# A conversion and two splits moved into a list scheduler's recurrence, two weight transposes moved to the host

## The chip, the core and the metric

One core of one Trainium2 chip runs the program. The metric is device time of one execution in microseconds (us). Engines are named as in the profile: PE is the matrix engine (TensorE), PEld its weight loads, DVE the vector engine, ACT the scalar engine, POOL the GpSimd engine, SP the engine that here only issues DMAs.

## The reference

Three layers follow one another, batch 4, 8 heads of 40 channels, 768 steps:

```python
# 1. recurrence, per batch and head, state 40 x 40
y[:, :, t] = einsum('bhd,bhde->bhe', r_t, state)
Sa = einsum('bhde,bhe->bhd', state, a_t)
state = state * w_t[:, :, None, :] - einsum('bhd,bhe->bhde', Sa, b_t) + einsum('bhd,bhe->bhde', v_t, k_t)
# x = y as [4, 768, 320]
# 2. four experts of causal attention (head dimension 64), the best two by x @ w_gate
out += mask_e * weight_e * (softmax(causal(q @ k.T / 8)) @ v @ wo[e])
# 3. gated MLP with a spatial product
h = maximum(x @ w_in, 0); u, v = h[..., :512], h[..., 512:]
vn = (v - mean(v)) / sqrt(var(v) + 1e-6)
return (u * (w_spatial @ vn + b_spatial)) @ w_out
```

w_in (320 x 1024) and w_out (512 x 320) arrive as float64; everything else is float32. The kernel receives the float64 arrays as 64-bit integers and makes float32 of them itself.

## The kernel before

**Recurrence.** `recurrence` works in 12 groups of 64 steps (group g, steps 2g and 2g+1 for the two halves of the batch). It describes each piece of work as an item: engine, assumed cost, due time, function, what it needs, the ring of buffers it takes from. `Plan.order` (line 53) is a list scheduler: it keeps a clock for each engine, looks at the items that could begin earliest, and of those takes the one with the smallest due time. What comes out is one order, in which all functions are called, so each engine's queue follows it. Items used below: `xo` (ACT issues the store of a solved block; the last one is ("xo", 11)), `gx` (SP loads G and R), `mb` (a product on PE), `mae`, `mbe`, `we`, `ue`, `ste`, `vte` (ACT's copies into G, xt, wsb, VU, s and vut), `u` (PE, line 324), `state` (DVE), `am` and `xs` (DVE; xs, line 418, makes the group's output), `out` (SP stores it to xd in DRAM, line 1072).

**Preparation in the tail.** Items of the plan know nothing of the attention weights. When ("xo", 11) has been issued, the early buffers are given back and a generator (`attn_prep`, line 600) is started: its first step issues all twelve loads of wq, wk, wv and w_gate on SP and a few small tiles; the rest, each a cast to a high part and a subtraction that leaves the low part, both on DVE (`split`, lines 586 to 593), is drawn eight steps at a time behind every `state`.

**Hand-over.** After the recurrence, `first_x` (line 727) loads the first batch's x as three tiles of 768 columns from xd (line 735) and splits them on DVE. Then attention and MLP of the four batches are written out in turns by `blend`, and the framework's scheduler sets the engines' order.

**First batch.** Beside attention(0) runs `rest`: `mlp_prep` and `wout_prep`. `mlp_prep` casts b_spatial (ACT) and takes its low part (POOL); loads wo and transposes it on PE into woT (line 680); for each of four column blocks of w_in loads three chunks (128, 128 and 64 rows of 256 columns), converts each with `load_f64`, multiplies by woT (line 691) and splits the result into wc_h and wc_l; for each of six row blocks of w_spatial transposes six 128 x 128 blocks on PE (line 703) and splits them from PSUM into ws_h and ws_l. All big inputs share one ring of four buffers, `big`. `wout_prep` converts four chunks of w_out (128 x 320) and splits them into wu_h and wu_l, the low part on POOL.

`load_f64` (line 557) is three words on ACT (scaled low word, sign, absolute value: lines 568, 569, 571), four integer or maximum forms on DVE (lines 572 to 575) and three products or sums on POOL (lines 576 to 578).

**Attention of a batch.** v for six row tiles (line 797, evicted into vv by ACT and DVE), then four heads e: projection (line 831), scores in blocks (first product line 859), maximum (DVE, 866), exponential (ACT, 871), scaling, transposes (901), product with vv (910, 912).

## Time and profile before

| what | us |
|---|---|
| median of three timed runs | 945.62 (943.25 to 946.6) |
| the profiled execution's own time | 940.45 |
| its span, first to last instruction | 938.7 |
| PE busy | 762.6 (81%) |
| DVE busy | 672.4 (72%) |
| ACT busy | 431.7 (46%) |
| POOL busy | 243.1 (26%) |
| first product of the first batch's attention | 404.44 |
| first product of the second batch's attention | 521.27 |
| mean granted clock of PE, share of full speed | 0.918 |

Times inside the execution count from the first instruction. A row's "idle before" names what ended the engine's idle time just before it. "issue" is time for which the profile shows no wait.

### The profile page before, as it was taken

How to read it: one execution, taken by the hardware profiler on the slowest of the kernel's cores; microseconds unless marked ns; L12 is line 12 of the kernel's file. 1: busy time of each engine (PE TensorE's matmuls, PEld its weight loads, DVE VectorE, ACT ScalarE, POOL GpSimd, SP SyncE). 2: the span in 40 equal slices, each digit the busy share in tenths (PEclk: the TensorE clock that was granted, in tenths of full speed). 3: DMA queues.
4: the chain of work that ended last, by engine and by line, in shares of the span. 5: the costliest groups of instructions: out<-in, count | busy, mean ns of one | idle time of the engine just before them, and what ended most of it. 6: DMA issues, size and time to landing. Idle time of an engine off the chain costs nothing.

```text
span 938.7 us, 29407 instructions
## 1 busy us (share of the span) xinstructions
PE 762.6 (81%) x12496; PEld 681.2 (73%) x12496; DVE 672.4 (72%) x1581; ACT 431.7 (46%) x1053; POOL 243.1 (26%) x425
## 2 busy tenths in 40 slices
PE   4615768968787878657887889998899988999898
PEld 4515667867676767645665779987799977999798
DVE  8999868889997943379988775576755767666730
ACT  2313433234343343136777554574655656555521
POOL 5652222232311010067810221111221113211041
PEclk9999898697989798868999989998899988999999
DMA  7956664677664352154101000010000100000001
GB/s 212 229 141 134 155 135 125 147 168 172 161 127 111 85 128 66 52 151 126 51 1 43 1 1 15 9 64 0 1 1 22 64 1 1 1 22 22 1 1 43
DMA packets 117669, 70.16 MB, mean 75 GB/s; under 512 B 100097, under 2 KB 103425, under 8 KB 117538
## 3 DMA queue, kind: packets, MB, share of 16 engines
q0 software_dynamic: 11520, 33.13, 12.5%
q1 hardware_dynamic: 54946, 25.71, 10.9%
q10 hardware_dynamic: 51072, 9.44, 5.5%
q8 instruction: 98, 1.61, 0.8%
q14 instruction: 33, 0.27, 0.1%
HBM read 50.95 MB, written 17.30 MB: 73 GB/s over the span
## 4 chain that ended last, share of the span: by engine, by line
PE 51%; DVE 27%; issue 7%; ACT 7%; DMA 4%; ACTq 1%; POOL 1%; SPq 1%; DVEq 0%; POOLq 0%
PE mm L942 6%; PE mm L943 6%; PE mm L944 5%; DVE sub L252 4%; PE mp L901 3%; DVE ls L254 3%; PE mp L831 3%; PE f L386 3%; PE pa L910 2%; PE f L411 2%; PE sc L859 2%; PE pa L912 2%; ACT f L871 2%; PE f L195 2%; DVE nm L866 2%
## 5 line engine op out<-in xcount | busy, mean ns | idle before, releaser
L871 ACT ACTIVATE f<-sc,nm 128x512 f32<-128x512 f32 (+3 forms) x128 | 68.9, 542 | 35.3 <-DVE nm L866 19.8
L195 PE MATMUL f<-at,kb 40*64 40x64 f32 x1536 | 41.4, 279 | 53.4 <-DVE kb L186 44.4
L592 DVE TENSOR_TENSOR ptl<-mp,pth 128x256 fp32r<-128x256 f32 (+2 forms) x144 | 65.3, 461 | 23.8 <-ACT pth L591 22.6
L866 DVE TENSOR_REDUCE nm<-sc 128x1 f32<-128x512 f32 (+3 forms) x128 | 63.4, 503 | 23.9 <-PE sc L864 20.1
L195 PEld LDWEIGHTS f<-at,kb 40*64 40x64 f32 x1536 | 37.2, 187 | 57.5 <-issue 29.6
L591 ACT CAST pth<-mp 128x256 fp32r<-128x256 f32 (+2 forms) x144 | 57.6, 410 | 36.3 <-PE mp L901 25.3
L252 DVE TENSOR_TENSOR sub<-ls 128x30 f32<-128x30 f32 (+9 forms) x180 | 59.5, 330 | 9.5 <-POOL ls L227 4.9
L910 PE MATMUL pa<-pth,vv 128*128 128x256 f32 x192 | 55.5, 302 | 11.8 <-DVE at L922 8.6
L254 DVE TENSOR_TENSOR ls<-ls,sub 128x30 f32<-128x30 f32 (+9 forms) x180 | 60.3, 335 | 6.6
L901 PE MATMUL mp<-ident,f 128*128 128x128 f32 x336 | 61.1, 301 | 2.9 <-DVE ptl L592 1.4
L912 PE MATMUL pa<-ptl,vv 128*64 128x256 f32 x192 | 52.2, 293 | 2.4 <-DVE ptl L592 1.9
L910 PEld LDWEIGHTS pa<-pth,vv 128*128 128x128 f32 x192 | 39.1, 204 | 18.9 <-DVE at L922 11.3
L386 PE MATMUL f<-rt,vut 64*64 64x64 f32 x1536 | 37.0, 249 | 17.0 <-issue 14.4
L391 DVE TENSOR_TENSOR am<-f,mask 128x1024 f32<-128x1024 f32 x24 | 29.2, 1222 | 29.5 <-PE f L386 29.4
L901 PEld LDWEIGHTS mp<-ident,f 128*128 128x128 f32 x336 | 43.5, 154 | 9.1 <-DVE f L887 3.1
L942 PE MATMUL mm<-ws_h,vn_h 128*128 128x384 f32 x144 | 49.9, 346 | 0.1
L859 PE MATMUL sc<-kk,qq 128*128 128x512 f32 (+3 forms) x128 | 44.5, 386 | 6.2 <-ACT f L871 4.7
L943 PE MATMUL mm<-ws_l,vn_h 128*128 128x384 f32 x144 | 49.1, 341 | 0.0
L944 PE MATMUL mm<-ws_h,vn_l 128*128 128x384 f32 x144 | 48.4, 336 | 0.0
L887 DVE TENSOR_SCALAR f<-f,sm 128x128 f32<-128x128 f32 (+2 forms) x96 | 44.3, 504 | 3.9 <-POOL sm L879 3.1
L386 PEld LDWEIGHTS f<-rt,vut 64*64 64x64 f32 x1536 | 33.0, 160 | 19.1 <-issue 16.1
L592 POOL TENSOR_TENSOR vn_l<-vr,vn_h 128x512 fp32r<-128x512 f32 x21 | 26.7, 1299 | 74.6 <-ACT vn_h L591 57.6
(230 smaller groups left out, 2325.5 us busy)
## 6 DMA issues: line engine op xcount, KB each, us to landing
xk<-in_x_dram POOLq DMA_DIRECT2D x48, 208.0 KB, 4.3
rt<-in_rt_dram POOLq DMA_DIRECT2D x24, 256.0 KB, 3.3
VU<-in_v_dram POOLq DMA_DIRECT2D x24, 256.0 KB, 5.1
xw<-in_x_dram POOLq DMA_DIRECT2D x24, 211.7 KB, 5.0
xa<-in_x_dram POOLq DMA_DIRECT2D x24, 208.0 KB, 4.5
xd<-xs SPq DMA_DIRECT2D x24, 160.0 KB
out_dram<-ob SPq DMA_DIRECT2D x24, 160.0 KB
lo<-la ACTq DMA_DIRECT2D x24, 128.0 KB
```

What stands on the lines that cost most here:

```text
L195: nc.tensor.matmul(pt[half(z ^ j), j, h * C:(h + 1) * C], KB[s][half(z, D), h, z ^ j], AT[s][half(z, D), h], start=(h == 0), stop=True, sk ...
L252: nc.vector.tensor_mul(tv, X[:, :m, j:j + 1].to_broadcast([m_, m, n]), X[:, j:j + 1, j + 1:].to_broadcast([m_, m, n]))
L254: nc.vector.tensor_sub(X[:, :m, j + 1:], X[:, :m, j + 1:], tv)
L386: nc.tensor.matmul(pa[half(j), h, i * C:(i + 1) * C], t[half(h), i, j * C:(j + 1) * C], RT[g][half(h), p, 2 * q2 + z], start=(i == 0), sto ...
L592: (lo_eng or nc.vector).tensor_sub(lo, src, hi.bitcast(F32))
L866: nc.vector.tensor_reduce(nm[:, z:z + 1], sc[:, :nn], op=OP.max, axis=AX.X, negate=True)
L871: nc.scalar.activation(pe[:, n0:n0 + nn], scs[z][:, :nn], AF.Exp, bias=nm[:, :1], accum_out=sm[:, z, i - i0:i - i0 + 1])
L901: nc.tensor.transpose(pp[:, j, z * 128:(z + 1) * 128], pes[z][:, (j0 + j) * 128:(j0 + j + 1) * 128], ident)
L910: nc.tensor.matmul(pa[:, c0:], vv[:, j0 + j, e].rearrange("p a h -> p (a h)"), pth[:, j, c0:], start=(j0 + j == 0), stop=False, skip_group ...
L942: nc.tensor.matmul(ps_, ah, bh, start=first, stop=False)
L943: nc.tensor.matmul(ps_, ah, bl_, start=False, stop=False)
L944: nc.tensor.matmul(ps_, al, bh, start=False, stop=last)
```

## The change

The conversion of w_in, the splits of the attention weights and the load and split of the first batch's x become items of the plan, with due times from 1000 up, so behind every item of the recurrence that could begin as early. w_in is read as eight chunks of 128 x 320 words of its flat form (`fl` on SP, `fw` on ACT, `fb` on DVE, `fo` on SP), and stored as float32 to `wif` in DRAM. The raw and the word tiles are two deep (FRB, FTB). x is loaded and split in four column groups of 192, each after the store of group 2, 5, 8, 11 (`xl`, `xh`, `xm`), all of them after all stores of wif ("sc"). The host transposes wo and w_spatial, so that `mlp_prep` loads woT directly and splits each w_spatial row block as 128 x 768 from SBUF. In `load_f64`, which only w_out still uses, and for w_out's low part, POOL's work goes to DVE.

```diff
+WB = 2
+FRB = 2
+FTB = 2
+XAT = (2, 5, 8, 11)
+XFB = 2
...
+       "s0": 1, "rt": 1, "vut": 2, "am": 2, "xs": 1, "wl": WB, "fl": FRB, "fw": FTB, "xf": XFB}
...
+REACH = {"xw": 4.5, "xa": 4.5, "xk": 4.5, "v": 5.5, "r": 5.5, "lo": 4.8, "l": 4.8, "xo": 4.5, "gx": 5.0, "init": 0.5, "wl": 3.0, "fl": 2.5, "fo": 2.5, "out": 3.0, "xl": 3.0}
...
+    if side is not None:
+        side(add, last, prep_stack.close)
     for name in plan.order():
         plan.items[name][3]()
-        if name == ("xo", last):
-            prep_stack.close()
-            prep = pre() if pre is not None else None
-        if prep is not None and name[0] == "state":
-            for _ in range(QPR):
-                next(prep, None)
...
-    nc.gpsimd.tensor_mul(m, m, e)
-    nc.gpsimd.tensor_add(t, t, m)
-    nc.gpsimd.tensor_mul(dst, t, sg)
+    nc.vector.tensor_mul(m, m, e)
+    nc.vector.tensor_add(t, t, m)
+    nc.vector.tensor_mul(dst, t, sg)
...
-    wo_sb = st.tile([128, 768], F32, name="big")[:, :2 * DM].rearrange("p (a d) -> p a d", a=2)
-    nc.sync.dma_start(wo_sb, wo.rearrange("(a e) h d -> (e h) a d", a=2))
...
-        for a in range(2):
-            nc.tensor.transpose(pt[:kn, a], wo_sb[:, a, k0:k0 + kn], ident)
-        nc.vector.tensor_copy(woT[:kn, k], pt[:kn].rearrange("p a e -> p (a e)"))
+    nc.sync.dma_start(woT[:, :2], wo[:256].rearrange("(k p) e -> p k e", p=128))
+    nc.sync.dma_start(woT[:64, 2], wo[256:])
...
-            load_f64(nc, st, nc.sync, w_in[k0:k0 + kn, f * 256:(f + 1) * 256], win[:kn, k], 256)
-            yield 1.0
+            nc.sync.dma_start(win[:kn, k], w_in[k0:k0 + kn, f * 256:(f + 1) * 256])
+        yield 1.0
...
-        for g in range(2):
-            pt = bank([128, 3, 128], MMB, "mm")
-            for s in range(3):
-                nc.tensor.transpose(pt[:, s], row[:, (3 * g + s) * 128:(3 * g + s + 1) * 128], ident)
-            ts = slice(t * 128, (t + 1) * 128)
-            split(ws_h[:, 3 * g:3 * g + 3, ts], ws_l[:, 3 * g:3 * g + 3, ts], pt)
-            yield 1.0
+        split(ws_h[:, t], ws_l[:, t], row)
+        yield 2.0
...
-        split(wu_h[:, a], wu_l[:, a], x, nc.gpsimd)
+        split(wu_h[:, a], wu_l[:, a], x)
...
+            add(("sb", 0), "SP", 0.3, next(due), begin, [("xo", last), ("x", 2 * last), ("x", 2 * last + 1)])
...
+                add(("wl", k), "SP", 0.4, next(due), lambda k=k: load_w(k), [("sb", 0)], makes="wl")
+                for n, cost in (("wv", 0.3), ("wq", 0.55)):
+                    add(("wh", n, k), "DVE", cost, next(due), lambda n=n, k=k: high(n, k), uses=[("wl", k)])
+                    add(("wo", n, k), "DVE", cost, next(due), lambda n=n, k=k: low(n, k), [("wh", n, k)], uses=[("wl", k)])
...
+            for i in range(len(src)):
+                add(("fl", i), "SP", 0.1, next(due), lambda i=i: load_f(i), [("sb", 0)], makes="fl")
+                for n in range(3):
+                    add(("fw", n, i), "ACT", 0.45, next(due), lambda i=i, n=n: word(i, n), [("fw", 0, i)] if n else [],
+                        makes="" if n else "fw", uses=[("fl", i)])
+                for n in range(7):
+                    add(("fb", n, i), "DVE", 0.36, next(due), lambda i=i, n=n: bits(i, n),
+                        [("fb", n - 1, i)] if n else [("fw", 1, i), ("fw", 2, i)] + ([("fb", 6, i - 1)] if i else []),
+                        uses=[("fw", 0, i)])
+                add(("fo", i), "SP", 0.1, next(due), lambda i=i: nc.sync.dma_start(dst[i], part[i][0]), [("fb", 6, i)],
+                    uses=[("fw", 0, i)])
+            add(("sc", 0), "SP", 0.1, next(due), second, [("fo", i) for i in range(len(src))] + [("wo", "wq", 2), ("wa", "wq", 2)])
...
+                add(("xl", r), "SP", 0.2, next(due), load_t, [("out", g), ("sc", 0)], makes="xf")
...
+    wo = given["moe_wo"]
+    given["moe_wo"] = wo.reshape(-1, wo.shape[-1]).T
+    given["moe2_w_spatial"] = given["moe2_w_spatial"].T
```

How the scheduler's order moves, in the places that the prediction speaks of. First ACT's queue around groups 9 and 10, from the copy of s for group 9 on (f64raw is a raw chunk of w_in; G, wsb, xt and VU belong to group 10). Before:

```order
212 L362 COPY s_6180<-f 128x320 x2
213 L376 COPY vut<-f 128x512 x4
214 L287 COPY G<-f 32x16x32 x2
215 L317 COPY wsb<-f 128x640
216 L299 COPY xt<-f 128x1024
217 L330 COPY VU_90<-f 64x16x40 x2
```

And in the change:

```order
212 L365 COPY s_6180<-f 128x320 x2
213 L1081 ACTIVATE f64t<-f64raw 128x320
214 L379 COPY vut<-f 128x512 x4
215 L1083 ACTIVATE f64m<-f64raw 128x320
216 L1085 ACTIVATE f64s<-f64raw 128x320
217 L290 COPY G<-f 32x16x32 x2
218 L1081 ACTIVATE f64t<-f64raw 128x320
219 L1083 ACTIVATE f64m<-f64raw 128x320
220 L1085 ACTIVATE f64s<-f64raw 128x320
221 L320 COPY wsb<-f 128x640
222 L302 COPY xt<-f 128x1024
223 L333 COPY VU_91<-f 64x16x40 x2
```

Six words of the first two chunks have come between the recurrence's own copies, the first of them ahead of vut.

Second, ACT's queue at head 0 of the first batch, up to the first exponentials (f,sm<-sc,nm; ws_h and wc_h are the high parts of w_spatial and of woT times w_in). Before:

```order
263 L834 ACTIVATE qq<-mp 64x512
264 L835 ACTIVATE qq<-mp 64x512
265 L568 ACTIVATE f64m<-f64raw 128x256
266 L834 ACTIVATE qq<-mp 64x256
267 L835 ACTIVATE qq<-mp 64x256
268 L568 ACTIVATE f64m<-f64raw 128x256
269 L871 ACTIVATE f,sm<-sc,nm 128x128
```

And in the change:

```order
276 L758 ACTIVATE qq<-mp 64x512
277 L759 ACTIVATE qq<-mp 64x512
278 L586 CAST wc_h<-mm 128x256
279 L586 CAST ws_h<-big 128x768 x2
280 L758 ACTIVATE qq<-mp 64x256
281 L759 ACTIVATE qq<-mp 64x256
282 L586 CAST ws_h<-big 128x768
283 L586 CAST wc_h<-mm 128x256 x2
284 L586 CAST ws_h<-big 128x768
285 L795 ACTIVATE f,sm<-sc,nm 128x128
```

The casts of w_spatial, of which two more stand a few rows higher, have moved from behind the first exponentials to ahead of them, and w_in's words are gone.

Third, SP's queue at the end of the recurrence and behind it (xd holds the groups' output, wif the converted w_in). Before:

```order
94 L1072 DMA xd<-xs 40x16x64 x6
95 L735 DMA xf<-xd 128x768 x2
96 L735 DMA xf<-xd 64x768
97 L665 DMA big<-in_moe_b_spatial_dram 1x768
```

And in the change:

```order
102 L1117 DMA wif<-f64t 128x320 x3
103 L996 DMA xd<-xs 40x16x64 x2
104 L1117 DMA wif<-f64t 128x320
105 L1130 DMA xf<-xd 128x2x192
106 L1131 DMA xf<-xd 64x192
...
111 L996 DMA xd<-xs 40x16x64 x2
112 L1130 DMA xf<-xd 128x2x192
113 L1131 DMA xf<-xd 64x192
114 L613 DMA big<-in_moe_b_spatial_dram 1x768
```

Three column groups of x are loaded between the last store of wif and the last store of xd, one behind it.

## Rows read from the trace of the kernel before

**Rows 1.** Busy table: stretch, length, PE, PEld, DVE, ACT, POOL, clock, DMA share, GB/s

```profile
345.00:396.00 51.00, 40.23 (x1531) 37.00 (x1529) 20.32 (x32) 16.14 (x28) 3.68 (x7) 0.87 0.29 69
404.00:479.30 75.30, 58.17 (x288) 45.15 (x288) 72.10 (x178) 50.84 (x143) 51.18 (x73) 0.85 0.31 91
479.30:497.70 18.40, 16.31 (x94) 13.04 (x94) 14.86 (x39) 12.51 (x36) 1.43 (x7) 0.91 0.13 44
```

**Rows 2.** Groups, DVE, 404 to 479.3: count, busy us, mean ns, idle before

```profile
L573 DVE TENSOR_SCALAR f64t<-f64t 128x256 int32<-128x256 int32 (+2 forms) x16 | 9.3, 579 | 0.2
...
L575 DVE TENSOR_SCALAR f64t<-f64t 128x256 int32<-128x256 int32 (+2 forms) x16 | 7.8, 489 | 0.1
...
L572 DVE TENSOR_SCALAR f64t<-f64t 128x256 f32<-128x256 f32 (+2 forms) x16 | 7.1, 444 | 0.1
...
L574 DVE TENSOR_SCALAR f64e<-f64t 128x256 int32<-128x256 int32 (+2 forms) x16 | 6.6, 414 | 0.1
...
L592 DVE TENSOR_TENSOR ws_l<-mm,ws_h 128x384 fp32r<-128x384 f32 x12 | 6.3, 543 | 0.8 <-ACT ws_h L591 0.7
...
L592 DVE TENSOR_TENSOR wc_l<-mm,wc_h 128x256 fp32r<-128x256 f32 x8 | 3.2, 415 | 0.1
...
L592 DVE TENSOR_TENSOR xh<-xf,xh 64x768 fp32r<-64x768 f32 x1 | 2.5, 2459 | 0.0
...
L592 DVE TENSOR_TENSOR xl<-xf,xh 128x768 fp32r<-128x768 f32 x2 | 1.9, 951 | 0.0
...
L589 DVE CAST xh<-xf 128x768 fp32r<-128x768 f32 (+1 forms) x3 | 1.7, 555 | 8.5 <-DMA xf<-xd 8.5
```

**Rows 3.** Timeline, 345 to 350, SP's issues and DVE: start, length, engine, line

```profile
345.02 0.50 SPq L620 DMA_DIRECT2D wvg<-in_moe_w_gate_dram  x1
...
345.57 0.73 SPq L619 DMA_DIRECT2D wqk<-in_moe_wq_dram  x1
...
349.25 0.30 DVE L589 CAST wv_h<-wvg 128x260 fp32r<-128x260 f32 x1 [1.52 <-DMA wvg<-in_moe_w_gate_dram]
```

**Rows 4.** Timeline, 345 to 356, group 10 on ACT and PE

```profile
345.10 2.05 ACT L376 COPY vut<-f 128x512 f32<-128x512 f32 x4 [5.62 <-PE f L369]
...
347.18 1.18 ACT L287 COPY G<-f 32x512 f32<-32x512 f32 x2
...
350.09 0.69 ACT L317 COPY wsb<-f 128x640 f32<-128x640 f32 x1 [1.73 <-PE f L312]
...
353.12 0.40 PE L294 MATMUL f<-R,G 64*64 64x64 f32 x12 [2.25 <-issue]
...
353.68 1.01 ACT L299 COPY xt<-f 128x1024 f32<-128x1024 f32 x1 [2.90 <-PE f L294]
...
355.91 1.95 PE L324 MATMUL f<-wsb,xt 64*64 64x40 f32 x64 [1.39 <-DVE xs L418]
```

**Rows 5.** Timeline's last xs, then the chain's rows to the last split

```profile
394.71 1.29 DVE L418 TENSOR_TENSOR xs<-f,pp 104x512 f32<-104x512 f32 x2 [2.58 <-PE f L411]
...
396.35 3.77 DMA xd<-xs
...
407.95 2.46 DVE xh L592
```

**Rows 6.** Timeline, ACT's cast of b_spatial

```profile
405.97 0.83 ACT L591 CAST bs<-big 1x768 fp32r<-1x768 f32 x1 [17.42 <-DMA big<-in_moe_b_spatial_dram]
```

**Rows 7.** Timeline, ACT, the word (Abs) of a 320-column chunk

```profile
441.69 0.51 ACT L571 ACTIVATE f64t<-f64raw 128x320 f32<-128x320 f32 x1
```

**Rows 8.** Groups, PE, 400 to 521, transposes of w_spatial

```profile
L703 PE MATMUL mm<-ident,big 128*128 128x128 f32 x36 | 5.9, 281 | 2.6 <-DVE wc_l L592 1.1 <-issue 0.9 <-DVE ws_l L592 0.5
```

**Rows 9.** Timeline, PE, first scores of heads 0, 2 and 3

```profile
434.18 1.31 PE L859 MATMUL sc<-kk,qq 128*128 128x128 f32 x3
...
482.18 0.95 PE L859 MATMUL sc<-kk,qq 128*128 128x128 f32 x3
...
499.67 0.67 PE L859 MATMUL sc<-kk,qq 128*128 128x128 f32 x3 [1.05 <-ACT qq L835]
```

More of the change, by code (lines that the diff above doesn't have):

```diff
@@ L648, in mlp_prep @@
     split = splitter(nc)
-    E, HD, DM = wo.shape
+    DM, EH = wo.shape
     S = w_sp.shape[0]
@@ L725, in x_tiles @@
     return kx.tile([128, 3, S], F32R, name="xh"), kx.tile([128, 2, S], F32R, name="xl")
-def first_x(tc, xd, kx, st, xs):
-    split = splitter(tc.nc)
-    _, _, DM, S = xd.shape
-    xs.append(x_tiles(kx, S))
-    xh, xl = xs[0]
-    for k, (k0, kn) in enumerate(chunks(DM)):
-        xf = st.tile([128, S], F32, name="xf")
-        tc.nc.sync.dma_start(xf[:kn], xd[0, 0, k0:k0 + kn, :])
-        for _ in range(XFW):
-            yield 0.5
-        split(xh[:kn, k], xl[:, k] if k < 2 else xh[64:, k], xf[:kn], None, True)
-        yield 0.5
 def moe_mlp(tc, xd, c, bank, E, HD, FF, out, ident, wk_, wk2, kx, x0, ml):
@@ L1091, in bank @@
                 return ps.tile(shape, F32, name=name, bufs=n)
-            xs = []
-            kx = stages["attn"].enter_context(tc.tile_pool(name="mwx", bufs=1, side="right"))
-            with tc.tile_pool(name="staging", bufs=3, side="right") as st:
-                for _ in first_x(tc, xd, kx, st, xs):
-                    pass
             k2 = stages["attn"].enter_context(tc.tile_pool(name="mwk", bufs=1, side="right"))
             k3 = stages["attn"].enter_context(tc.tile_pool(name="mwk2", bufs=2, side="right"))
-            attention, mlp, prog = moe_mlp(tc, xd, c, bank, E, HD, FF, out, ident, k2, k3, kx, xs[0], ml)
+            attention, mlp, prog = moe_mlp(tc, xd, c, bank, E, HD, FF, out, ident, k2, k3, c["kx"], c["x0"], ml)
             wp = stages["attn"].enter_context(tc.tile_pool(name="mwu", bufs=1, side="right"))
@@ L1105, in rest @@
                 with tc.tile_pool(name="staging2", bufs=STC) as st:
-                    yield from mlp_prep(tc, cp, st, bank, c, wo, w_in, w_sp, b_sp, w_out, ident)
+                    yield from mlp_prep(tc, cp, st, bank, c, wo, wif, w_sp, b_sp, w_out, ident)
                     yield from wout_prep(tc, wp, st, c, w_out)
```

169 lines of the change are left out of this document (110 added, 59 removed).

## The prediction

> All times below are microseconds of the one profiled execution unless said otherwise. Its span is 938.7 and its own time 940.45; the median of the three timed runs is 945.62, so this execution is 5.17 below the median. The sum is made against 940.45, and the same difference is then taken off 945.62.
>
> **What bounds the kernel now.** I read the busy table by stage first, because the shares of the whole span hide that the program has parts with different limits. From 404.0 to 479.3, where the first batch's attention runs beside the preparation of the MLP weights, VectorE (DVE) is busy 72.10 of 75.30, that is 96%, and TensorE (PE) 58.17; in the next stretch, with the preparation over, DVE is at 14.86 of 18.40 (81%) and PE at 16.31 (89%) [rows 1]. So DVE is the limit exactly as long as the preparation lasts. In the last 51 of the recurrence it is the other way round: DVE 20.32, ACT 16.14, PE 40.23 [rows 1]. The grouped lines then say what fills DVE in the middle stage [rows 2], the timeline how the recurrence's last groups hang together [rows 3, 4], and the rows around the last store show the hand-over [rows 5, 6].
>
> **Part 1, the conversions in the recurrence's tail.** In the kernel before, the attention weights' splits stood on DVE ahead of xs(8), and the product u(10) waited 1.39 for that [rows 4]. The change puts xs(8) ahead of the splits, so up to 1.4 is gained. On ACT the first Abs of the float64 words now stands ahead of vut(9), and the copies of G and wsb for group 10 come after the rest of that chunk (the first piece of the order). Its load leaves where the third weights' load left SP, at 345.57 [rows 3]. How long it takes to land is not in the trace; the nearest rows are those of the second weights' load, whose last piece left at 345.02 and whose cast began at 349.25, 4.2 later [rows 3]. So the Abs, 0.51 long [rows 7], ends near 350.3, and vut(9), which began at 345.10, starts there: vut 2.05 to 352.4, two more words to 353.4, the two G copies 1.18 to 354.6, mb(10) about 1.2 to 355.8, the second chunk's three words on ACT meanwhile (to 356.1), wsb 0.69, xt 1.01, u(10) at 358.0 against 355.91 [rows 4]: **+2.1**. If the pause of 2.25 inside mb(10), put down to issue [rows 4], comes again, it is +4.4; if the load lands in time, -1.4.
>
> The Trainium skill, page "DMA: Bandwidth & Descriptors", section "Anatomy of one DMA — SWDGE (gpsimd) path", has a fixed 2.0 us plus the bytes at 436 GB/s for a DMA that GpSimd issues. For this chunk's 320 KB that is an estimate of 2.75; by it u(10) would come at 356.6, and the whole sum below would be -12.2 instead of -10.8. The weights' load with its 4.2, issued from SP, does not agree, and the measurement is taken.
>
> On SP, group 11's loads of G and R now stand behind two more chunk loads, which wait for ACT's first six words; by the working above those are over at 356.1, and the G and R loads had to wait for mb(10) until 355.8 anyway: nothing. On POOL only a small memset is added. The 24 words on ACT (0.51 each) are 12, the 56 operations on DVE about 26 (32 shift forms of 0.45 and 24 products of 0.5, by their 256-column forms [rows 2]); ACT has 35 idle and DVE 31 in that window [rows 1], so the work costs nothing. If this cover is gone, it is through waiting, and that is a rival below. Of the first batch's x, three of four column groups are loaded behind the last store of the converted w_in, so around xs(11). Ahead of xs(11) stand six of their operations: twice half of a 0.555 cast and of a 0.951 subtraction, and once a quarter of both, 1.9 [rows 2]. DVE was idle 2.58 just before xs(11) [rows 5], so they fit if the data is there. I take **+1.0**, between 0 and 3.8 (the work twice over, if the second group's load is late). The recurrence ends **3.1 later**, between -1.4 and +8.2.
>
> **Part 2, from the last store to the second head's end.** Now the last store takes 3.77 to land, and the last split of x ends at 410.41, that is 10.3 after the landing at 400.12 [rows 5]. With the change only 192 columns are left, about 1.2 on DVE. But vv(0) will not come at once: ACT casts b_spatial ahead of it, whose load is issued behind x, and that cast began at 405.97, 5.9 after the landing [rows 6]. So the hand-over gives some 4, which the stage can use only as far as DVE lets it. I therefore price the stage as a whole, in two ways.
>
> *By work.* DVE's float64 operations are 9.3 + 7.8 + 7.1 + 6.6 = 30.8 for 16 chunks [rows 2]; w_in's twelve have 12 x 256 columns of 12 x 256 + 4 x 320, so 0.706 of it: -21.8. First x: 2.5 + 1.9 + 1.7, less 1.2: -4.9. The split of w_spatial: 6.3 before, now six of 0.951: -0.6 [rows 2]. From POOL come w_out's three products and its subtraction, 16 operations of 320 columns, some 0.5 each by 0.415 for 256 [rows 2]: +8.0. DVE is left with 72.1 - 19.3 = 52.8. PE loses 36 transposes, 5.9 [rows 8], and six of wo, about 1.0 by the same, and keeps 58.2 - 6.9 = 51.3. The host's transposing costs no device time and the bytes loaded stay the same. With PE as busy as it is undisturbed, 89% [rows 1], the stage lasts 57.9 instead of 75.3: **-17.4**. That is the good end; it leaves out waits.
>
> *By waits.* All six casts of w_spatial's rows now stand on ACT ahead of the first exponential (the second piece of the order), and later rows load into buffers which w_in's products must free first. So I let head 0 start no sooner after the last store than now. From head 0's first scores (434.18) to head 2's (482.18) are 48.0; an undisturbed head takes 499.67 - 482.18 = 17.5 [rows 9], two take 35.0, and some late w_out operations on DVE may add 2.6: **-10.4**. That is the poor end.
>
> I take the middle, **-13.9**: w_in's twelve loads and w_spatial's six stay in a row on SP, which speaks against the good end; DVE's queue holds little old work once head 0 runs, which speaks against the poor one. From head 2 on nothing moves that later batches wait for; I cost that at nothing.
>
> **Sum:** 3.1 - 13.9 = **-10.8**, 940.45 to 929.65, and for the median 945.62 to **934.8**. With the bounds of both parts: 8.2 - 10.4 = -2.2 (943.4) and -1.4 - 17.4 = -18.8 (926.8).
>
> **The rivals.**
>
> *POOL was the brake.* Beside POOL's products, DVE's four float64 operations of like shapes take from 0.414 to 0.579 on average [rows 2]. If POOL slows all of DVE's work there, DVE falls well under PE, and the stage comes down to PE's own 51.3: -24.0 + 3.1 = -20.9, **924.7**. For it: that spread. Against it: the products, casts and maxima keep depending on each other across engines, and 89% was the best share of PE nearby. Chance 0.17. The Trainium skill, page "SBUF — State Buffer", section "Who interferes with whom", says that VectorE and GpSimd share one port pair as an exclusive lock; the spread agrees with that.
>
> *No change.* w_spatial's fourth row needs the buffer of w_in's last column block, whose product needs accumulators that the casts and subtractions of wc free, and these stand in ACT's and DVE's queues among w_out's operations. If the last row lands 7 later than I allow, the stage gives 3.4 and the recurrence takes 3.1 back: **945.3**. For it: ACT's order. Against it: w_in arrives converted, so its products come sooner. That the conversions don't fit in the tail and only trade places would give about the same. Chance 0.13.
>
> *Slower: ACT held at each pair of chunks.* A chunk's tiles are two deep, so the words of chunks 2 and 3, 4 and 5, 6 and 7 wait for a store to land, and the recurrence's own copies stand behind them on ACT. A store took 3.77 [rows 5]. If each of the three pairs holds the path that long (11.3), on top of the 4.4 and 3.8 of part 1, the recurrence ends 19.5 later and 13.9 comes back: +5.6, **951.2**. It decides from the point where the tail loses more than 13.9. For it: SP sends the stores behind G's loads, which wait for PE. Against it: ACT has 35 idle, and the planner spreads the words. Chance 0.11.
>
> **How the numbers follow.** My forecast has 0.59, the rivals 0.17, 0.13 and 0.11. The range may leave out 2 in 10: from 922 (the first rival and a little) to 948 (no change, and the milder part of the last). Faster or slower counts from 0.3%, 2.8, about what a measurement of this kernel can tell from no change: faster is my forecast and the first rival, 0.76; the same 0.13; slower 0.11.
>
> **What would show it.** Right: in the changed profile the last xs starts 2 to 5 after 394.71, with ACT idle ahead of vut(9) on f64raw's load; vv(0) follows b_spatial's cast; head 2's first scores stand near 471 (482.18 + 3.1 - 13.9); DVE is under 90% in the middle stage and POOL has no float64 operation. Wrong: ACT idle for several microseconds before the words of later chunks (the slower rival), or before casts of w_spatial's rows at head 0 (no change), or head 2's scores before 465 (the first rival).

## The result, and the profile after

| | before | the change |
|---|---|---|
| median, us | 944.45 (943.25 to 946.6, four runs) | 931.42 (926.51 to 938.09, four runs) |
| ratio | | 0.9871, 95% interval 0.9828 to 0.9914 |
| the profiled execution's own time | 940.45 | 938.09 |
| its span | 938.7 | 936.4 |
| PE, DVE, ACT, POOL busy | 762.6, 672.4, 431.7, 243.1 | 758.5, 676.4, 429.6, 202.7 |

The time falls by 1.3% (0.9 to 1.7). Each ratio is taken against its own set's runs of before and is not the quotient of the two medians (in e1's set 0.993, where the medians give 0.996). The profiled execution of the change is its slowest of four, so its span is only 2.3 below before's. Spans of single executions tell little here: ACT's queue is the same in every kernel of this study up to group 9's copy of s, and yet that copy starts anywhere from 333.45 to 345.56 in their profiles. I therefore cut each profile at three instructions and compare the stretches behind the first: the *tail*, from that copy to the start of the last xs; the *stage*, from there to the first product of v of the second batch (521.11 in before, 516.30 in the change); the *rest*, to the end. Start, tail, stage and rest add up to the span.

| profile of | start | tail | stage | rest | ratio to before (95% interval) |
|---|---|---|---|---|---|
| before | 338.73 | 55.98 | 126.40 | 417.59 | |
| the change | 340.40 | 63.83 | 112.07 | 420.10 | 0.9871 (0.9828 to 0.9914) |
| e1_again | 345.56 | 59.57 | 110.75 | 419.82 | 0.9930 (0.9899 to 0.9961) |
| e2_host_only | 338.22 | 53.83 | 127.30 | 418.05 | 0.9997 (0.9978 to 1.0016) |
| e3_no_conversion | 342.82 | 52.98 | 126.72 | 418.18 | 1.0018 (0.9994 to 1.0042) |
| e4_true_latency | 333.45 | 58.15 | 111.77 | 416.93 | 0.9859 (0.9826 to 0.9892) |
| e5_w_out_pool | 344.54 | 62.22 | 110.72 | 417.12 | 0.9931 (0.9899 to 0.9963) |
| e6_conversion_on_dve | 342.16 | 52.92 | 123.19 | 417.63 | 0.9956 (0.9922 to 0.9989) |
| e7_vv_elsewhere | 338.78 | 55.10 | 111.23 | 416.89 | 0.9835 (0.9795 to 0.9875) |
| e8_loads_on_pool_queue | 340.12 | 56.31 | 115.42 | 420.15 | 0.9900 (0.9856 to 0.9944) |
| e9_products_on_dve_alone | 342.10 | 54.67 | 125.17 | 416.76 | 1.0019 (0.9986 to 1.0053) |
| e10_x_behind_last_xs | 336.43 | 59.32 | 113.32 | 417.43 | 0.9924 (0.9893 to 0.9956) |
| e11_transposes_on_pe | 341.20 | 58.79 | 105.08 | 417.63 | 0.9875 (0.9834 to 0.9916) |
| e12_fewer_loads | 337.07 | 55.70 | 116.63 | 417.00 | 0.9891 (0.9855 to 0.9927) |

In the first pair of profiles the change loses 7.9 in the tail and gains 14.3 in the stage.

**The tail.** The changed kernel's timeline of ACT around groups 9 and 10 answers to [rows 4] (start, length, engine, line, operation; in brackets the idle time ahead and what ended it):

```profile
340.40 0.75 ACT L365 COPY s<-f 128x320 f32<-128x320 f32 x2 [0.39 <-PE f L405]
352.23 0.49 ACT L1081 ACTIVATE f64t<-f64raw 128x320 f32<-128x320 f32 x1 [11.07 <-DMA f64raw<-in_moe_w_in_dram]
352.62 2.03 ACT L379 COPY vut<-f 128x512 f32<-128x512 f32 x4
...
355.45 1.17 ACT L290 COPY G<-f 32x512 f32<-32x512 f32 x2
...
357.92 0.69 ACT L320 COPY wsb<-f 128x640 f32<-128x640 f32 x1
359.26 1.01 ACT L302 COPY xt<-f 128x1024 f32<-128x1024 f32 x1 [0.65 <-PE f L297]
363.09 1.39 ACT L333 COPY VU<-f 64x640 f32<-64x640 f32 x2 [2.81 <-PE f L327]
```

ACT stands 11.07 for the first chunk's load, issued at 345.93, with vut(9) behind it. From the copy of s to vut(9) are 12.22, against 6.37 before. But VU(10), the copy behind u(10), comes only 3.5 later than before on that scale (22.69 against 19.18), so part of the wait is made up; the other 4.3 of the tail's 7.9 lie behind VU(10).

The changed kernel's timeline of DVE at the end of the recurrence, which answers to the first of [rows 5]:

```profile
399.10 1.23 DVE L394 TENSOR_TENSOR am<-f,mask 128x1024 f32<-128x1024 f32 x1 [1.50 <-PE f L389]
401.46 0.36 DVE L1135 CAST xh<-xf 128x384 fp32r<-128x384 f32 x1 [1.14 <-DMA xf<-xd]
401.86 0.56 DVE L1140 TENSOR_TENSOR xl<-xf,xh 128x384 fp32r<-128x384 f32 x1
402.69 0.25 DVE L1135 CAST xh<-xf 64x192 fp32r<-64x192 f32 x1 [0.28 <-DMA xf<-xd]
402.98 0.35 DVE L1140 TENSOR_TENSOR xh<-xf,xh 64x192 fp32r<-64x192 f32 x1
403.36 0.36 DVE L1135 CAST xh<-xf 128x384 fp32r<-128x384 f32 x1
403.76 0.56 DVE L1140 TENSOR_TENSOR xl<-xf,xh 128x384 fp32r<-128x384 f32 x1
404.23 1.28 DVE L421 TENSOR_TENSOR xs<-f,pp 104x512 f32<-104x512 f32 x2
```

Six operations on x stand between the last am and the last xs, and the first waits 1.14 for its load. From am to xs are 5.13; before, the same two are 3.81 apart.

**The stage.** The busy table from the last xs to head 2's first scores, for before:

```profile
394.71:482.18 87.47, 59.92 (x297) 46.75 (x298) 75.55 (x183) 52.39 (x146) 53.22 (x79) 0.84 0.31 92
```

and for the change, the whole, head 0 and head 1 (the columns are those of [rows 1]):

```profile
404.23:475.73 71.50, 51.91 (x256) 41.54 (x256) 52.65 (x148) 39.82 (x105) 13.04 (x27) 0.81 0.28 87
431.81:459.82 28.01, 19.43 (x72) 14.32 (x73) 22.30 (x62) 14.94 (x39) 3.41 (x7) 0.70 0.13 42
459.82:475.73 15.91, 13.20 (x84) 10.29 (x84) 13.43 (x36) 11.69 (x35) 1.43 (x7) 1.00 0.01 2
```

DVE's busy time falls from 75.55 to 52.65, and its share from 86% to 74%. Neither engine is near the share it reached before (96% and 89% [rows 1]): PE is at 73%. In head 0 PE was granted 0.70 of its full clock on average, that is time at both levels, 1.2 and 2.4 GHz; in head 1 it had 1.00. First scores of heads 0, 1 and 2 in the change, as in [rows 9]:

```profile
431.81 0.67 PE L783 MATMUL sc<-kk,qq 128*128 128x128 f32 x3 [1.01 <-ACT qq L759]
...
459.82 0.67 PE L783 MATMUL sc<-kk,qq 128*128 128x128 f32 x3 [0.68 <-ACT qq L759]
...
475.73 0.67 PE L783 MATMUL sc<-kk,qq 128*128 128x128 f32 x3 [1.03 <-ACT qq L759]
```

Measured from the last xs, head 0 starts after 27.58 (39.47 before) and head 2 after 71.50 (87.47). Head 0 itself takes 28.01, head 1 15.91. Why head 0 is slow shows on ACT:

```profile
411.31 0.83 ACT L586 CAST bs<-big 1x768 fp32r<-1x768 f32 x1 [15.91 <-DMA big<-in_moe_b_spatial_dram]
412.98 0.65 ACT L586 CAST vv<-mp 128x256 fp32r<-128x256 f32 x2 [0.83 <-DMA woT<-in_moe_wo_dram]
...
439.88 0.83 ACT L586 CAST ws_h<-big 128x768 fp32r<-128x768 f32 x1
440.62 0.36 ACT L795 ACTIVATE f<-sc,nm 128x128 f32<-128x128 f32 x1
```

The first two rows are the hand-over: vv(0) behind b_spatial's cast [rows 6]. The last two: the first exponential starts 8.81 after the first scores, right behind the sixth cast of a row of w_spatial. In between, ACT waits 1.23 for w_spatial's loads and 2.58 for products of wc on PE, each time ahead of a cast in that queue.

### The profile page after: what moved, and what is told of

Read it like the earlier page. It is cut to its first block, busy times and chain, and to the rows that moved or that the text cites. A ratio compares the mean times of both kernels' runs of the same rounds, so it can differ in the third digit from the quotient of the medians.

```text
span 936.4 us, 29275 instructions
## 1 busy us (share of the span) xinstructions
PE 758.5 (81%) x12454; PEld 681.1 (73%) x12454; DVE 676.4 (72%) x1605; ACT 429.6 (46%) x1035; POOL 202.7 (22%) x374
## 4 chain that ended last, share of the span: by engine, by line
PE 53%; DVE 22%; issue 8%; DMA 7%; ACT 6%; POOL 2%; SPq 1%; ACTq 0%; DVEq 0%; POOLq 0%
PE mm L866 6%; PE mm L867 6%; PE mm L868 5%; PE mp L755 4%; PE mp L825 3%; PE f L389 3%; DVE sub L255 2%; PE f L198 2%; ACT f L795 2%; DVE ls L257 2%; PE pa L834 2%; PE pa L836 2%; PE sc L783 2%; PE f L344 2%; DVE ptl L587 2%
## 5 line engine op out<-in xcount | busy, mean ns | idle before, releaser
L795 ACT ACTIVATE f<-sc,nm 128x512 f32<-128x512 f32 (+3 forms) x128 | 69.0, 542 | 37.6 <-DVE nm L790 18.7
L834 PEld LDWEIGHTS pa<-pth,vv 128*128 128x128 f32 x192 | 40.6, 211 | 15.8 <-DVE at L846 9.8
L801 POOL TENSOR_SCALAR sm<-sm 128x2 f32<-128x2 f32 x48 | 11.7, 244 | 150.4 <-ACT f L795 143.7
L785 PE MATMUL sc<-kk,ql 128*128 128x512 f32 (+3 forms) x128 | 43.1, 356 | 0.1
```

What stands on the lines that cost most here:

```text
L795: nc.scalar.activation(pe[:, n0:n0 + nn], scs[z][:, :nn], AF.Exp, bias=nm[:, :1], accum_out=sm[:, z, i - i0:i - i0 + 1])
L834: nc.tensor.matmul(pa[:, c0:], vv[:, j0 + j, e].rearrange("p a h -> p (a h)"), pth[:, j, c0:], start=(j0 + j == 0), stop=False, skip_group ...
```

## The experiments

Theory A at the outset: the tail loses by waiting for the first chunk's load, and the stage gains because DVE's work was its limit. Rivals: B, the tail loses by added work; C, POOL was the brake in the stage.

### e1_again: the change once more

No edit. 

> The changed kernel unchanged, for a second profile and more times. In its first profile the last xs starts at 404.23, 9.5 later than before, head 2's first scores at 475.73, 6.5 earlier, and the end is 2.3 earlier; of its four times (926.5 to 938.1) the profiled one is the longest. Theory A (the loss in the tail is a wait for a chunk's load, whose landing varies): this profile's time is shorter where the idle time of ACT ahead of the first word (11.07 in the first profile) is shorter, and the last xs starts between 397 and 403. Theory B (the tail loses by added work, the same in every execution): last xs again within 1 of 404.2, and the times differ behind batch 1's start (516.3). Median 931 by both, 928 to 935.

Measured: 935.14 (924.81 to 938.25), before 938.79 in the same set, ratio 0.993. Tail 59.57 instead of 63.83, with ACT idle 9.79 instead of 11.07, and stage 110.75. The last xs starts at 405.13, which is what theory B expected by the clock and not what A did, but the execution was 5.2 late ahead of the tail, so the clock decides nothing. On the scale of the tail A is borne out in part: of the 4.3 by which the tail is shorter, 1.7 lie ahead of VU(10), where the load acts, and the rest behind it, which A doesn't explain. In the profiles of kernels with this order of words (the change, e1, e5, e10, e11) the word starts 6.3, 4.1, 5.6, 4.0 and 3.5 after the first chunk load was issued (in e5 the profile names another load, of VU, as what ended the wait).

### e2_host_only: the transposes alone

Against the kernel before, and as in the change:

```diff
-            nc.tensor.transpose(pt[:kn, a], wo_sb[:, a, k0:k0 + kn], ident)
-        nc.vector.tensor_copy(woT[:kn, k], pt[:kn].rearrange("p a e -> p (a e)"))
+    nc.sync.dma_start(woT[:, :2], wo[:256].rearrange("(k p) e -> p k e", p=128))
+    nc.sync.dma_start(woT[:64, 2], wo[256:])
...
-                nc.tensor.transpose(pt[:, s], row[:, (3 * g + s) * 128:(3 * g + s + 1) * 128], ident)
+        split(ws_h[:, t], ws_l[:, t], row)
...
+    given["moe2_w_spatial"] = given["moe2_w_spatial"].T
```

> The kernel before with the transposes of wo and w_spatial on the host alone. It takes 36 + 6 transposes from PE (6.9) and three copies of woT and some of the split from DVE (about 2). If DVE's own work is the limit of the stage, as the prediction has it, about -2 against before (ratio 0.998, 0.995 to 1.000). Rival, that PE's order or the accumulators are what the stage waits for: -5 to -7 (ratio 0.993 to 0.995).

Measured: ratio 0.9997 (0.9978 to 1.0016), stage 127.30. The rival's 0.993 to 0.995 is excluded. The first expectation is not: 0.9997 is at the edge of its 0.995 to 1.000, and the interval can't tell its -2 from nothing. So 6.9 of PE's work and the copies are worth 2 at most here.

### e3_no_conversion and e6_conversion_on_dve: w_in back beside the first batch

Against the change; e3 besides has the three products of `load_f64` and w_out's subtraction on POOL again, e6 leaves them on DVE:

```diff
-            nc.sync.dma_start(win[:kn, k], w_in[k0:k0 + kn, f * 256:(f + 1) * 256])
+            load_f64(nc, st, nc.sync, w_in[k0:k0 + kn, f * 256:(f + 1) * 256], win[:kn, k], 256)
...
-                add(("fl", i), "SP", 0.1, next(due), lambda i=i: load_f(i), [("sb", 0)], makes="fl")
...
-                    yield from mlp_prep(tc, cp, st, bank, c, wo, wif, w_sp, b_sp, w_out, ident)
+                    yield from mlp_prep(tc, cp, st, bank, c, wo, w_in, w_sp, b_sp, w_out, ident)
```

> The change without the conversion of w_in in the tail: w_in is converted beside the first batch as before, POOL's part on POOL as before; the weights' and x's items and the host's transposes stay. By the terms on record the stage keeps DVE's 21.8 for w_in and loses the 8.0 that came from POOL, so it is about 14 longer than in the change, and the tail is shorter by what the conversion costs there. If that is the whole 8 between the two profiles (9.5 less 1.3 of lateness from ahead of the tail), the time is 931.4 + 14 - 8 = 937; if the conversion costs nothing in the tail, 945; if the stage is not DVE's, 927 or less. Last xs near 396 by the first, near 403 by the second.

> The change with the conversion of w_in back beside the first batch, as in the run without conversion in the tail, but all of w_in's and w_out's products on DVE: against that run 48 products and 4 subtractions leave POOL, some 20 to 22 more for DVE, which was busy in 73.4 of the 87.0 of the stage there. If DVE's own work is the limit, the stage is 15 to 22 longer than 87.0 and the time 1.7 to 2.4% above before. If POOL was the brake (its products hold DVE's, or the chain over POOL is what lasts), the stage stays within 5 of 87.0 or falls and the time is within 0.6% of before.

Measured: e3 1.0018, e6 0.9956. In e3 the tail is 52.98, so the conversion is what lengthens it, and the stage is as long as before: x's and the weights' items and the host's part bring nothing while DVE still converts. In e6 DVE does 52 operations more than in e3, and nothing gets longer; e6's interval (0.9922 to 0.9989) even lies below e3's (0.9994 to 1.0042), so beside the other parts of the change the release of POOL is worth some 0.6%. Against e3 the change is surely faster, against e6 not by the timed runs: 0.9899 to 0.9961 in e1's set overlaps e6's interval. The busy tables from the last xs to head 2, and for head 0 alone, e3:

```profile
395.80:482.83 87.03, 56.85 (x256) 45.95 (x256) 73.37 (x173) 51.70 (x141) 55.58 (x79) 0.78 0.28 84
422.94:466.88 43.94, 25.28 (x97) 19.12 (x97) 42.11 (x90) 27.48 (x72) 34.42 (x42) 0.79 0.30 93
```

e6, to head 2:

```profile
395.08:480.01 84.93, 58.58 (x256) 45.97 (x256) 72.06 (x225) 52.10 (x141) 13.19 (x27) 0.76 0.27 86
```

DVE's busy time is 73.37 and 72.06. With the conversion beside the first batch the stage to head 2 is long where DVE is busy long, but that busy time isn't the sum of what its operations take alone. In e3 head 0 starts 27.14 after the last xs, as early as in the change, and nothing comes of it: DVE is then busy in 42.11 of head 0's 43.94, and head 2 starts after 87.03, as before. An earlier start is a gain only because the conversion is gone from DVE.

### e9_products_on_dve_alone: one part by itself

Against the kernel before:

```diff
-    nc.gpsimd.tensor_mul(m, m, e)
-    nc.gpsimd.tensor_add(t, t, m)
-    nc.gpsimd.tensor_mul(dst, t, sg)
+    nc.vector.tensor_mul(m, m, e)
+    nc.vector.tensor_add(t, t, m)
+    nc.vector.tensor_mul(dst, t, sg)
...
-        split(wu_h[:, a], wu_l[:, a], x, nc.gpsimd)
+        split(wu_h[:, a], wu_l[:, a], x)
```

> The kernel before with one part of the change alone: the 48 float64 products and sums and w_out's 4 subtractions go from POOL to DVE. If DVE's own work is the limit of the stage: 20 more on DVE, ratio to before 1.015 to 1.022. If POOL is the brake, as the pair of runs without conversion in the tail has it (DVE's shift and mask forms took 0.38 to 0.52 with the products on POOL, 0.28 with them on DVE): ratio 0.993 to 0.997, DVE's busy time from the last xs to head 2's first scores within 3 of the 75.6 of before although it does 52 operations more.

Measured: ratio 1.0019, 0.9986 to 1.0053: neither the +2% nor the gain. DVE's busy time stays within 3 of before's, as the rival had it. The busy table from the last xs to head 2's first scores, and the grouped lines of DVE there, in which the last four answer to [rows 2]:

```profile
396.77:483.97 87.20, 59.86 (x297) 48.33 (x297) 76.70 (x236) 52.62 (x147) 10.79 (x27) 0.80 0.30 92
```

```profile
L577 DVE TENSOR_TENSOR f64t<-f64t,f64m 128x256 f32<-128x256 f32 (+2 forms) x16 | 7.0, 435 | 0.0
L576 DVE TENSOR_TENSOR f64m<-f64m,f64e 128x256 f32<-128x256 f32 (+2 forms) x16 | 6.8, 425 | 0.0
...
L572 DVE TENSOR_SCALAR f64t<-f64t 128x256 f32<-128x256 f32 (+2 forms) x16 | 4.7, 296 | 0.0
L575 DVE TENSOR_SCALAR f64t<-f64t 128x256 int32<-128x256 int32 (+2 forms) x16 | 4.5, 284 | 0.0
L573 DVE TENSOR_SCALAR f64t<-f64t 128x256 int32<-128x256 int32 (+2 forms) x16 | 4.5, 283 | 0.1
L574 DVE TENSOR_SCALAR f64e<-f64t 128x256 int32<-128x256 int32 (+2 forms) x16 | 4.5, 280 | 0.0
```

The four shift, mask and maximum forms fall from 30.8 together to 18.2 (4.7 + 4.5 + 4.5 + 4.5) when POOL no longer makes the products beside them; L573's mean goes from 579 to 283 ns. The products, the sums and w_out's subtraction cost DVE 22.5 in all. DVE's busy time ends 1.15 above before's, and the stage to head 2 at 87.20 against 87.47. 12.6 of the 22.5 come back in these four forms. Over all rows of DVE the sum rises by 6.3 only, since other rows are shorter too; and rows overlap in time, their sum being 11.0 above the busy time in before and 16.1 above it in e9, which takes up the rest. So the brake of rival C is there, and by itself its release pays for the moved work, no more.

### e5_w_out_pool: w_out's part back on POOL

Against the change, the same lines the other way round:

```diff
-    nc.vector.tensor_mul(m, m, e)
+    nc.gpsimd.tensor_mul(m, m, e)
...
-        split(wu_h[:, a], wu_l[:, a], x)
+        split(wu_h[:, a], wu_l[:, a], x, nc.gpsimd)
```

> The change with w_out's three float64 products and its subtraction back on POOL, 16 operations that the prediction priced at +8.0 of DVE's work. If DVE's work is what the stage lasts by, the stage (last xs to head 2's first scores, 71.5 and 71.1 in the two profiles of the change) falls by 6 to 8 and the time with it. If the stage of the change waits (DVE is busy in 52.65 of its 71.5, PE in 51.9), nothing: within 2. If POOL slows DVE or lengthens w_out's chain: 2 to 6 longer.

Measured: 0.9931, as the change's 0.993. To head 2 are 72.26, against 71.50 and 71.06, and DVE is busy in 53.65 of it with 16 operations fewer than in the change's 52.65. The same as in e9: of the term of 8.0 nothing is seen, neither in busy time nor in the stage.

### e4_true_latency: the planner told longer landings

Against the change, three figures of REACH:

```diff
-"wl": 3.0, "fl": 2.5, "fo": 2.5
+"wl": 5.0, "fl": 6.5, "fo": 4.0
```

> The change with the planner told longer landings: 5.0, 6.5 and 4.0 for the weights' loads, the chunks' loads and stores instead of 3.0, 2.5 and 2.5 (the first profile shows 6.3 for the first chunk). The first word then stands behind vut(9). Theory A (ACT's wait of 11.07 ahead of the word is what the tail loses): vut(9) comes back to 346 to 347 and the last xs to 396 to 399, the time falls by 4 to 6, to 926. Theory B (added work): last xs within 2 of 404, the time within 1.5 of the change's. By a third way the last chunks are over later, since each pair of buffers turns over more slowly, and x is loaded behind the last xs: last xs early but first scores late, time as in the change or up to 3 longer.

Measured: 925.16 (921.44 to 931.79), ratio 0.9859; the interval lies below that of the change in the same set. The planner now puts the first word behind vut(9) and G, and all pieces of x behind the last xs. Timeline of ACT:

```profile
333.45 0.75 ACT L365 COPY s<-f 128x320 f32<-128x320 f32 x2
341.74 2.05 ACT L379 COPY vut<-f 128x512 f32<-128x512 f32 x4 [7.54 <-PE f L372]
...
345.00 0.49 ACT L1081 ACTIVATE f64t<-f64raw 128x320 f32<-128x320 f32 x1
```

and of DVE at the end:

```profile
388.53 1.22 DVE L394 TENSOR_TENSOR am<-f,mask 128x1024 f32<-128x1024 f32 x1
...
391.60 1.29 DVE L421 TENSOR_TENSOR xs<-f,pp 104x512 f32<-104x512 f32 x2 [0.85 <-PE f L414]
398.03 0.56 DVE L1135 CAST xh<-xf 128x384 fp32r<-128x384 f32 x1 [5.14 <-DMA xf<-xd]
```

ACT no longer waits for a load there, and from am to xs are 3.07. The tail is 58.15 here and 55.10, 56.31 and 55.70 in e7, e8 and e12, which share its order: 56.3 on average, against 61.1 for the four with the change's order (the change, e1, e5, e11). But two waits went at once here. Of these 4.8, 2.1 lie ahead of VU(10) (19.6 after the copy of s instead of 21.7), where theory A has them, and 2.8 behind the last am (3.1 instead of 5.9), where the pieces of x stood. Theory A thus explains less than half of what the tail gets back. The third way of the expectation shows too, though not in the time: head 0 starts 35.81 after the last xs instead of 27.6, and head 2 after 73.76 instead of 71.50 and 71.06. The rest of the fall in time lies behind head 2, where the stage and the rest together are 5.2 shorter on average than in the two profiles of the change; the cause of that is open.

### e10_x_behind_last_xs: the two waits apart

Against the change:

```diff
-                    add(("xh", r, k), "DVE", cost, next(due), lambda k=k, f=high_t: f(k), uses=[("xl", r)])
+                    add(("xh", r, k), "DVE", cost, next(due), lambda k=k, f=high_t: f(k), [("xs", last)], uses=[("xl", r)])
```

> The change with all splits of the first batch's x behind the last xs on DVE; the words of the float64 chunks stay where they are. In the three profiles with the change's tail the last xs starts 5.1 to 6.1 behind the last am, in before's order 3.81. If the pieces of x make that difference, it goes back to 3.8 and the tail (from group 9's copy of s to the last xs, 59.6 to 63.8 with the change) loses 1.3 to 2.3; the rest of its excess over before's 54.9, some 5, stays and belongs to the words on ACT. The time falls by up to 2, or not at all if the splits are then late for vv.

Measured: from am to xs 3.78 again, tail 59.32; the ratio, 0.9924, is the change's in e1's set (0.993). Timeline of DVE:

```profile
391.97 1.23 DVE L394 TENSOR_TENSOR am<-f,mask 128x1024 f32<-128x1024 f32 x1 [0.25 <-PE f L389]
395.75 1.29 DVE L421 TENSOR_TENSOR xs<-f,pp 104x512 f32<-104x512 f32 x2 [2.55 <-PE f L414]
```

The start of head 0 is 33.11 after the last xs instead of 27.6, so what the tail gains the hand-over gives back, and no gain in time can be seen. Of the tail's excess over before's order 4.5 stay, as expected.

### e7_vv_elsewhere and e12_fewer_loads: two attempts at the stage

Against e4; the first piece is in both, the second in e12 alone:

```diff
-            k2 = stages["attn"].enter_context(tc.tile_pool(name="mwk", bufs=1, side="right"))
             k3 = stages["attn"].enter_context(tc.tile_pool(name="mwk2", bufs=2, side="right"))
+            k2 = stages["attn"].enter_context(tc.tile_pool(name="mwk", bufs=1, side="right"))
```

```diff
-            nc.sync.dma_start(win[:kn, k], w_in[k0:k0 + kn, f * 256:(f + 1) * 256])
+        nc.sync.dma_start(win[:, :2], w_in[:256, fs].rearrange("(k p) f -> p k f", p=128))
+        nc.sync.dma_start(win[:64, 2], w_in[256:, fs])
```

> The version with the longer landings told to the planner, and the two pools of the attention's buffers opened in the other order, so that vv doesn't lie where the pieces of x were. In the changed kernel's profile the first cast of vv (412.98) follows the end of x's last split (412.9). If that shared memory is what holds vv, the first vv cast comes 3 to 8 earlier against the last xs and the time falls by 1 to 4 against the version with longer landings (ratio to before 0.982 to 0.985). If it is b_spatial's cast or the products of wc ahead of v's on PE, nothing: ratio 0.986 as there.

> The fastest version so far (longer landings, vv elsewhere: 0.9835), with each column block of the converted w_in loaded by two DMAs instead of three, eight in place of twelve. At 0.59 each on SP, w_out's and w_spatial's loads leave 2.4 earlier. If the preparation waits for SP's issues: 1 to 2.5 faster, ratio 0.981 to 0.983. If it waits for buffers and queues behind them: ratio 0.983 to 0.985.

Measured: e7 923.74, ratio 0.9835, the fastest of all; e12 0.9891. In e7 the first vv follows v's products:

```profile
402.11 0.84 ACT L586 CAST bs<-big 1x768 fp32r<-1x768 f32 x1 [14.11 <-DVE xh L1140]
403.30 0.37 ACT L586 CAST vv<-mp 128x256 fp32r<-128x256 f32 x1 [0.36 <-PE mp L721]
```

That is 9.4 after the last xs instead of 15.8 in e4. But the stage is 111.23 against 111.77, so the earlier vv brings nothing that can be seen there, although the ratio lies in the range expected for a gain; the intervals of e4 and e7 overlap. Fewer loads don't help either; 0.9891 fits neither expectation. The stage is then 5.4 longer, of which 4.1 lie behind head 2; why is left open.

### e8_loads_on_pool_queue: SP relieved

Against e4:

```diff
-            nc.sync.dma_start(win[:kn, k], w_in[k0:k0 + kn, f * 256:(f + 1) * 256])
+            nc.gpsimd.dma_start(win[:kn, k], w_in[k0:k0 + kn, f * 256:(f + 1) * 256])
```

> The version with longer landings, and the twelve loads of the converted w_in issued by POOL instead of SP, on which they take 7.04 in the changed kernel's profile, with w_spatial's and w_out's loads behind them. If SP's row of issues is what the preparation waits for, w_out's and w_spatial's loads leave 5 to 7 earlier against the last xs, head 2's first scores come 2 to 6 earlier and the time is 0.980 to 0.984 of before. If the rows of w_spatial wait for buffers anyway, or POOL's issues land later, nothing or up to 3 longer: 0.985 to 0.990.

Measured: 0.990 against e4's 0.9859, with overlapping intervals, so no gain. The framework's scheduler moved more than the loads: on ACT w_out's words now stand ahead of the first vv and wait for their own loads:

```profile
410.15 0.49 ACT L563 ACTIVATE f64m<-f64raw 128x320 f32<-128x320 uint32 x1 [4.77 <-DMA f64raw<-in_moe_w_out_dram]
...
412.91 0.50 ACT L563 ACTIVATE f64m<-f64raw 128x320 f32<-128x320 uint32 x1 [1.49 <-DMA f64raw<-in_moe_w_out_dram]
...
416.42 0.49 ACT L563 ACTIVATE f64m<-f64raw 128x320 f32<-128x320 uint32 x1 [2.25 <-DMA f64raw<-in_moe_w_out_dram]
...
419.24 0.64 ACT L586 CAST vv<-mp 128x256 fp32r<-128x256 f32 x2
```

The first vv comes 22.8 after the last xs, 15.8 in e4. Whether SP's row of issues costs anything by itself is not answered by this.

### e11_transposes_on_pe: the host's part undone

Against the change, the lines of e2_host_only the other way round:

```diff
+            nc.tensor.transpose(pt[:kn, a], wo_sb[:, a, k0:k0 + kn], ident)
...
+                nc.tensor.transpose(pt[:, s], row[:, (3 * g + s) * 128:(3 * g + s + 1) * 128], ident)
...
-    given["moe2_w_spatial"] = given["moe2_w_spatial"].T
```

> The change without the host's part: wo and w_spatial are transposed on PE again, 42 transposes (6.9) and three copies of woT. The prediction priced the host's part at -6.9 of PE's work. If PE's work counts in the stage, the time is 5 to 7 longer than the change's (ratio to before 0.998 to 1.000 where the change has 0.993). If PE and DVE wait there anyway (each busy in 73% of the stage), within 2 of the change.

Measured: 925.44 (923.77 to 928.44), ratio 0.9875; neither expectation. Its stage is 105.08, 5.7 to 7.0 *shorter* than the change's, though PE does 42 transposes more. ACT's timeline:

```profile
430.49 0.37 ACT L806 ACTIVATE f<-sc,nm 128x128 f32<-128x128 f32 x1 [0.34 <-DVE nm L801]
...
435.81 0.48 ACT L586 CAST ws_h<-mm 128x384 fp32r<-128x384 f32 x1
```

and the busy table of heads 0 and 1:

```profile
426.91:448.61 21.70, 17.77 (x105) 13.84 (x103) 20.33 (x60) 15.01 (x43) 2.25 (x7) 1.00 0.24 73
448.61:466.07 17.46, 14.42 (x98) 11.52 (x96) 15.18 (x42) 13.97 (x40) 1.43 (x7) 1.00 0.00 1
```

The rows of w_spatial must now pass through PE's accumulators, and in the new order their casts stand behind the first four exponentials instead of ahead of all; the first exponential comes 3.6 after the first scores (426.91), not 8.8. Head 0 takes 21.70 instead of 28.01, and PE was granted its full clock throughout, where the change had 0.70. How much of the 6.3 is order and how much clock, the run doesn't separate. Head 2's first scores come 66.08 after the last xs, against 71.06 to 75.69 in the eight profiles with w_spatial transposed on the host and w_in converted in the tail. But early casts alone don't bring the first exponential: in e4 all six are over 1.5 after head 0's first scores, and it still comes 7.3 after them, with a wait of 2.07 for DVE's maximum. By the timed runs alone e11 is not surely faster than the change: 0.9834 to 0.9916 against 0.9899 to 0.9961.

## Why the prediction was right, and where not

**The total.** 934.8 was forecast, 931.42 came, inside the range. By ratio the forecast was -1.14% (934.8 against 945.62); measured were -1.3% and, in e1's set, -0.7%. The way of the change is right, the size is in part luck. Put together from the profiles, the terms are, on the averages below, +6.3 in the tail (forecast +3.1), -16.2 to head 2 (-13.9), and +1.2 and +2.4 behind head 2, which I had at nothing: -6.3, or -0.7%, as in e1's set. That is 4.5 short of the forecast: the stage's surplus of 2.3 hides a part of the 6.8 by which the tail and the stretch behind head 2 were too cheap. By e1's interval (-0.4% to -1.0%) the forecast is too high; it meets the first set.

**The tail: right in one term, short in two.** Forecast +3.1. The four profiles with the change's tail average 61.1, the three of kernels with before's order (before, e2, e9) 54.8: +6.3, inside the bounds of -1.4 to +8.2. Term by term, on these averages:

- Abs ahead of vut(9), priced at +2.1 for u(10). VU(10) comes 21.7 after the copy of s, 19.5 before: +2.1. From the load's issue to the word are 3.5 to 6.3, around the 4.2 taken. The Trainium skill's fixed 2.0 plus bytes at 436 GB/s (page "DMA: Bandwidth & Descriptors", section "Anatomy of one DMA — SWDGE (gpsimd) path"), an estimate of 2.75 for another issuing engine, lies below all five.
- The pieces of x ahead of xs(11), priced at +1.0: from am to xs are 5.9 instead of 3.7, +2.2. The six operations take 2.4 where the data is there, instead of the 1.9 taken, and "they fit if the data is there" failed: DVE waits 1.1 to 2.7 for the first group's load. In e3, where the loads don't wait for a conversion, three of the four groups are split by 374, and from am to xs are 3.5. The upper bound of 3.8 covered it.
- The words and bits of chunks 2 to 7, "the work costs nothing": from VU(10) to the last am are 33.5 instead of 31.6, +1.9; in e3 and e6, whose tails have no conversion, they are 31.5 and 31.3. Idle time enough on ACT and DVE did not make them free. That am and the copies each stand behind single operations of half a microsecond by then is a likely reason, not a shown one. e4's order does not cure this (33.6 on average in its four profiles).

**The stage: right in size, by a different route.** Forecast -13.9 between -17.4 and -10.4; to head 2 it is 71.50 and 71.06 instead of 87.47, -16.0 and -16.4. From the last xs to head 2 DVE loses 22.9 of busy time and PE 8.0; forecast were 19.3 and 6.9. (The forecast's 52.8 and 51.3 left over belong to the stretch from 404.0 to 479.3, so that the measured 52.65 and 51.91 meet them by a different stretch.) But three steps failed:

- "I let head 0 start no sooner." It starts 11.9 sooner after the last xs, and that is where most of the gain stands; e3 shows that it is one only with the conversion gone from DVE. The two heads, which were to take 37.6, take 43.9. The very rows that I named for that bound, the six casts of w_spatial ahead of the first exponential, hold head 0 in the change's order; e11, where they stand behind it, takes 6.3 less there, with the clock as a part that is not separated.
- "From POOL come ... +8.0" was mis-sized: e5 and e9 measure nothing. A row of DVE's time beside a busy POOL is not the price of the operation alone, and so the 21.8 for w_in (21.7 by its own figures) also held waiting.
- PE's -6.9 for the transposes was credited in the good end and is worth 2 at most (e2); in the change e11 makes it likely that the order turns it into a loss, but by the timed runs that is not sure.

**From head 2 on** I priced nothing. In two profiles of the change the rest is 2.2 to 2.5 longer than before's 417.59; in e5, e10 and e11 it is not (417.12 to 417.63), with small differences in the order of PE. The cause is left open.

**The rivals.** *POOL was the brake*: the spread that spoke for it was real (e9), but by itself the time is not to be had, since the work goes to the engine that is relieved; beside the other parts some 0.6% is (e6 against e3). The Trainium skill's exclusive lock on the port pair ("SBUF — State Buffer", "Who interferes with whom") agrees with 579 against 283 ns; its page "Perfetto Trace Analysis", section "Optimizing Scalar/DVE Operations", adds that moving work between GpSimd and DVE might not help, and in e9 it does not (1.0019). *No change* is what the parts alone give (e2, e3, e9). *ACT held at each pair of chunks*: the idle times ahead of later words are 2.24 and 0.31 in all in the change's profile.

**The signs.** The last xs was to start 2 to 5 after 394.71 and starts 9.5 after: missed. ACT idle on f64raw's load ahead of vut(9), DVE under 90%, POOL without float64 work: seen. vv(0) behind b_spatial's cast: seen, 0.84 after its end, and 0.08 after the end of the last split of x, in whose memory vv lies; in e7, with vv elsewhere, it starts 5 ahead of that split, but the stage is no shorter. Head 2's scores came at 475.73, not near 471, because the last xs was 9.5 late, of which 1.7 came from ahead of the tail. Of the signs of being wrong, ACT's idle time ahead of casts of w_spatial's rows at head 0 is 1.23, not several.

## What to carry to other kernels

When work is moved into a list scheduler's gaps, check what the planner believes of a load's landing: the word that waits for it holds everything behind it on its in-order engine, and longer landings in the plan were worth more here (0.993 to 0.986, by this and by x's pieces going behind the last xs) than moving 22.5 us of work between engines (1.002). Price an operation from a stretch in which the engine that slows it (here POOL beside DVE) is quiet, or the busy time of a saturated engine will count the same waiting twice. A term that comes out right in the sum is not yet a right term: here errors of opposite sign met. And a step that is made cheaper can move ahead of the critical one: look in the new order for what now stands between the first scores and the first exponential.

The version with the lowest ratio is e7, 923.74 against 939.14 in its set (0.9835); its interval overlaps those of e4 and e11. e7 with the transposes on PE was not run.
